# The first reading of k and v for their bounds: flat 2 KB rows in place of rows by key and head

## The chip, the cores and the metric

The kernel runs on one core of one Trainium2 chip. The metric is the device time of one execution in microseconds (us); of several runs the median is given.

## What is computed

```python
def _attn_ref(q, k, v, f):
    B, H, S, D = q.shape                      # 4, 8, 576, 64
    scores = np.matmul(q, k.transpose(0, 1, 3, 2)) / np.sqrt(D)
    cum = np.cumsum(np.log(np.clip(f, 0.0001, 1.0)), axis=-1)
    scores = np.where(causal, -1e9, scores + cum[..., :, None] - cum[..., None, :])
    attn = softmax(scores)
    return np.matmul(attn, v)

def _moe_ref(x, w_in, w_out):                 # 2304 x 512, 512 x 2048, 2048 x 512
    h = x @ w_in
    return (h * np.tanh(np.log1p(np.exp(h)))) @ w_out

def _moe2_ref(x, w_in, w_out, g_ln):          # d_ff 1024
    h = x @ w_in
    solu = h * softmax(h)
    return (layernorm(solu) * g_ln) @ w_out

def reference(...):
    x = _attn_ref(q, k, v, f).transpose(0, 2, 1, 3).reshape(B * S, H * D)
    return _moe2_ref(_moe_ref(x, ...), ...)
```

All is in float32. The kernel splits each operand of a product into a high and a low part in float16, scaled by a power of two that comes from a bound on the operand, and adds three products.

## The kernel before, in words

Three stages run one into the other. The attention goes batch by batch (`b` 0 to 3), in five chunks `i` of up to 128 queries each and in groups of heads; one step takes a group through scores (PE, L436 to L441), maximum and exponential (DVE L483 and L496, ACT L485, L499, L500), the split into two float16 parts (`step_h`, L523 and L524), a DMA transpose `pT<-ph` (L529) and the product with v (PE, L555 to L557). The first feed-forward layer takes blocks of 256 tokens as they come out: `up` (PE, L785), the activation (`mish_a`, `mish_b`, `mish_c`), `down` (PE, L829). The second layer (`Stage2`) starts when the last attention step is issued; its products are L1028 and L1068. Each batch has 576 keys; batches 1 to 3 lie in the 128-row chunks with an offset of 64, so that chunk 0 has 64 rows there and chunk 4 has 128.

The scale of a batch's k and v must be known before its first chunk is split, so k and v are read twice. The first reading is for the bounds alone: for each chunk `c` a load (`load_raw(b + 1, c, "kv")`), and an activation Square with a running sum on ACT (`stats`, L316), which writes one column of the small tile `st`; `scales` (L332) takes the maximum over the columns, adds over the partitions with a product by ones (L329), and forms the scales. The second reading loads q, k and v of a chunk again (`load_raw(nb, ni, "qkv")`) for the split (`split_k`, `split_v`, `split_q`). Batch 0 is read once, into other buffers.

`load_raw` (L292) puts one key into one partition: from the array [batch, head, key, 64] it takes, for each of up to 128 keys, eight pieces of 64 floats (256 bytes), one per head:

```python
            i = nc.sync.dma_start(
                t[r0:r1_].rearrange("p (h d) -> p h d", h=H),
                src[b, :, t0:t0 + n, :].rearrange("h s d -> s h d"),
            )
```

The tiles of both readings come from one pool, `rawp`, with three buffers of 128 x 512 floats that go round in the order of the program; a load waits until the tile three before it has been used. `ahead` (L645) places the loads of the first reading of batch `b + 1` in the attention of batch `b`, at the steps n = 6, 8, 14, 15, 16 counted over heads and chunks from chunk 2 on, and the Squares at n = 8, 10, 15, 16, 17; `scales` follows at n = 18.

All loads, stores and transposes are issued from SP's queue, in order. A scheduler sets each engine's row of instructions from the program's order, the dependences and its own estimates of durations; inside an engine the row is kept at run time.

Of the kernel before, what the change touches and what calls it, by code (L numbers as in the profile page):

```python
# [8 lines left out]
F32 = mybir.dt.float32  # L9
# [3 lines left out]
AF = mybir.ActivationFunctionType  # L13
# [5 lines left out]
P = 128  # L19
B, H, S, D = 4, 8, 576, 64  # L20
DM = H * D
# [52 lines left out]
def rows_of(b, c):  # L74
    off = OFF[b]
    lo = max(128 * c, off)
    hi = min(128 * c + 128, off + S)
    return lo - 128 * c, hi - 128 * c, lo - off
# [130 lines left out]
def emit(tc, q, k, v, f, w_in, w_out, w2_in, w2_out, g_ln, out):  # L209
    nc = tc.nc  # L210
# [39 lines left out]
    rawp = ea.enter_context(tc.tile_pool(name="rawp", bufs=RB, side="right"))  # L250
# [35 lines left out]
    raw = {}  # L286
    sc = {}
# [4 lines left out]
    def load_raw(b, c, which, pool=None):  # L292
        r0, r1_, t0 = rows_of(b, c)
        n = r1_ - r0
        for nm in which:
            src = {"q": q, "k": k, "v": v}[nm]
            if pool is None:
                t = rawp.tile([P, DM], F32, tag="raw", name=f"raw{nm}_{b}_{c}")
            else:
                t = pool.pop()  # L300
            raw[nm, b, c] = t
# [3 lines that stand above are left out]
            )  # L305
        return i

    def stats(b, c, which):

        if ("st", b) not in sc:  # L310
            sc["st", b] = att.tile([P, 2, NCH], F32, tag="st", name=f"st_{b}", bufs=2)
            nc.vector.memset(sc["st", b], 0.0)
        r0, r1_, _ = rows_of(b, c)
        for nm in which:
            jk = attd.tile([P, DM], F32, tag="x32", name=f"jk{nm}_{b}_{c}", bufs=1)
            nc.scalar.activation(  # L316
                jk[r0:r1_], raw[nm, b, c][r0:r1_], AF.Square,
                accum_out=sc["st", b][r0:r1_, "kv".index(nm), c:c + 1])
# [13 lines left out]
    def scales(b, which):  # L332

        j0 = "kv".index(which[0])
        n = len(which)
        t = att.tile([P, 6, 2], F32, tag="sct", name=f"sct{which}_{b}", bufs=1)
        x = [t[:, i, :n] for i in range(6)]
        nc.vector.tensor_reduce(x[0], sc["st", b][:, j0:j0 + n], axis=AX.X, op=ALU.max)
        src = across(x[0], x[1])
        nc.vector.tensor_scalar(x[1], src, 2.0 ** -40, None, op0=ALU.max)  # L340
        root2(nc, x[4], x[1])
        nc.vector.reciprocal(x[5], x[4])
        for i, nm in enumerate(which):
            pw, ip = t[:, 4, i:i + 1], t[:, 5, i:i + 1]
            if nm == "k":
                u = att.tile([P, 2], F32, tag="scu", name=f"scu_{b}", bufs=2)
                c = 64.0
                nc.vector.tensor_scalar(u[:, 0:1], pw, 0.125 / c, None, op0=ALU.mult)
                nc.vector.tensor_scalar(u[:, 1:2], ip, c, None, op0=ALU.mult)
                sc["q", b], sc["k", b] = u[:, 0:1], u[:, 1:2]  # L350
            else:
                u = att.tile([P, 1], F32, tag="scv", name=f"scv_{b}", bufs=2)
                nc.vector.tensor_scalar(u, ip, 2.0 ** 14, None, op0=ALU.mult)
                nc.vector.tensor_scalar(iv[b], pw, 2.0 ** -14, None, op0=ALU.mult)
                sc["v", b] = u
# [9 lines left out]
    def split_k(b, c):  # L365
        r0, r1_, t0 = rows_of(b, c)
        n = r1_ - r0
        t = kn[cnt["kn"] % KNB]
        cnt["kn"] += 1
        t3 = t[:, :H * P].rearrange("p (h d) -> p h d", h=H)  # L370
        rk = hd(raw["k", b, c][r0:r1_])
        s = sc["k", b][r0:r1_]
        split(nc, t3[r0:r1_, :, 64:], t3[r0:r1_, :, :64], rk, s, qmode(b, c, 0))
        kc = ktr[:, (b * NCH + c) % NKT]
        kt[b, c] = kc
        nc.sync.dma_start_transpose(out=kc[:, :H, r0:r1_], in_=t[r0:r1_, :H * P])
        nc.vector.tensor_copy(kc[:64, H:, r0:r1_], kc[64:, :H, r0:r1_])
        nc.sync.dma_start(
            kc[64:67, H:, r0:r1_],
            dd[b * H:(b + 1) * H, :, t0:t0 + n].rearrange("h j s -> j h s"),  # L380
        )

    def split_v(b, c):
        r0, r1_, _ = rows_of(b, c)
        vc = attd.tile([P, 2, DM], F16, tag="vt", name=f"vt_{b}_{c}", bufs=6)
        vt[b, c] = vc
        rv = raw["v", b, c][r0:r1_]
        s = sc["v", b][r0:r1_]
        split(nc, vc[r0:r1_, 0], vc[r0:r1_, 1], rv, s, qmode(b, c, 1))

    def split_q(b, c):
        r0, r1_, t0 = rows_of(b, c)
        t = attd.tile([P, H, P], F16, tag="qn", name=f"qn_{b}_{c}", bufs=1)
        rq = hd(raw["q", b, c][r0:r1_])
        s = sc["q", b][r0:r1_]
        split(nc, t[r0:r1_, :, :64], t[r0:r1_, :, 64:], rq, s, qmode(b, c, 2))
        qa = attd.tile([P, H, P], F16, tag="qa", name=f"qa_{b}_{c}", bufs=2)
        pend["qt"] = nc.sync.dma_start_transpose(out=qa[:, :, r0:r1_], in_=t[r0:r1_].rearrange("p h d -> p (h d)"))
        qb_ = qb[cnt["qb"] % 2]
        cnt["qb"] += 1  # L400
        nc.vector.tensor_copy(qb_[:64, :, r0:r1_], qa[:64, :, r0:r1_])  # L401
        qt[b, c] = (qa, qb_)
# [242 lines left out]
    def ahead(b, i, h):  # L645

        nb, ni = (b, i + 1) if i + 1 < NCH else (b + 1, 0)
        if b + 1 < B and i in (2, 3, 4):
            n = (i - 2) * H + h
            if n in (6, 8, 14, 15, 16):  # L650
                load_raw(b + 1, (6, 8, 14, 15, 16).index(n), "kv")
            if n in (8, 10, 15, 16, 17):
                stats(b + 1, (8, 10, 15, 16, 17).index(n), "kv")
            if n == 18:
                scales(b + 1, "kv")
        if nb < B:
            if h == (LD if ni else 3) and nb > 0:
                load_raw(nb, ni, "qkv")
            if h == LD and nb == 0 and ni >= 3:
                load_raw(nb, ni, "q")  # L660
            if h == (LD + 2 if ni else 4):
                if nb or ni > 1:
                    split_k(nb, ni)
                    split_q(nb, ni)
                split_v(nb, ni)
# [20 lines left out]
    def slot_pe():  # L686
        n = pos["k"]
        if n < len(seq):
            step_s(*seq[n])
            b, i, hs = seq[n]  # L690
            for h in hs:
                ahead(b, i, h)
        pvs(n - LAG)
        pos["k"] += 1
# [10 lines left out]
    for x in range(len(order) + WPF):  # L705
        if WPF <= x < len(order):
            wsteps.append((order[x][0].load, order[x][1]))
        if x >= WPF:
            w, n = order[x - WPF]
# [28 lines left out]
    for c in range(NCH):  # L738
        stats(0, c, "k")
# [9 lines left out]
    for c in range(NCH):  # L749
        stats(0, c, "v")  # L750
# [124 lines left out]
    for j in range(NBLK):  # L875
        last = (j + 1) * TB - 1
        b, t = divmod(last, S)
# [28 lines left out]
    for hn in range(2 * (NF + 5)):  # L906
        n, half = divmod(hn, 2)
# [212 lines left out]
```

## Time and profile before

| | |
|---|---|
| median of 3 runs | 859.61 us (858.01 to 860.01) |
| profiled execution | span 856.0 us from the first to the last instruction; its own time is not listed, the median is 3.6 us above its span |
| busy PE, DVE, ACT, POOL | 739.0, 617.6, 548.2, 440.8 us |
| DMA | 328568 packets, 114.83 MB, 317676 of them under 512 bytes |
| mean granted clock of TensorE | 0.977 of full speed |

Busy times are of one engine each and overlap. A busy PE is not a PE at its peak. The DMA share of a stretch is the mean busy share of 16 DMA engines; it can pass 1 where packets overlap. In the chain of waits each piece is what released the next one; "issue" is time in which an engine waited for nothing that the profile shows. SPq is SP's queue, which issues DMAs.

### The profile page before, as it was taken

To read this page: it belongs to the slowest core of one execution; us is meant where nothing else is said; L and a number is where in the kernel's file an instruction comes from. 1 tells how busy PE (TensorE), PEld (TensorE's weight loads), DVE (VectorE), ACT (ScalarE), POOL (GpSimd) and SP (SyncE) were. 2 spreads that over 40 slices of the span, in tenths; PEclk is the share of its full clock that TensorE was granted. 3 is DMA by queue.
4 is the path that set the end of the run, shared out by engine and by line. 5 is a ranking of instruction groups with operands and counts; after the bars stand their busy time and mean duration, and the time that the engine had idled before them with its cause. 6 is when DMAs were issued, how large, how long until landed. Compare 5 with 4: busy or idle time off the path is not lost.

```text
span 856.0 us, 15746 instructions
## 1 busy us (share of the span) xinstructions
PE 739.0 (86%) x5822; PEld 456.4 (53%) x5822; DVE 617.6 (72%) x1158; ACT 548.2 (64%) x1202; POOL 440.8 (51%) x341
## 2 busy tenths in 40 slices
PE   0545776689999999997999999986999999999998
PEld 0334543447656666575666767553555554444443
DVE  6799999498867989769896755599566444665551
ACT  5645647868779877877877767686855554333331
POOL 2268676755976667755678653128832222022110
PEclk9999997889999999999999999999999999999999
DMA  9999555477899898988897533941013323344443
GB/s 239 229 215 281 160 176 94 93 137 145 153 174 190 168 169 153 184 155 153 173 180 119 115 70 63 233 156 61 26 38 87 74 64 73 87 101 106 104 88 82
DMA packets 328568, 114.83 MB, mean 134 GB/s; under 512 B 317676, under 2 KB 317676, under 8 KB 328492
## 3 DMA queue, kind: packets, MB, share of 16 engines
q1 hardware_dynamic: 328492, 113.84, 63.9%
q8 instruction: 45, 0.74, 0.4%
q14 instruction: 31, 0.25, 0.1%
HBM read 46.59 MB, written 9.55 MB: 66 GB/s over the span
## 4 chain that ended last, share of the span: by engine, by line
PE 37%; DVE 24%; DMA 12%; ACT 11%; issue 8%; POOL 6%; SPq 1%; DVEq 0%; ACTq 0%; POOLq 0%
PE h L1028 11%; PE o L1068 10%; PE x L829 7%; PE h L785 6%; DMA pT<-ph 3%; POOL ph L524 3%; DVE th L806 2%; DVE ta L802 2%; ACT p L485 2%; DVE ph L521 1%; DMA w2i_r<-in_moe_w_in_dram 1%; DMA ktr<-kn 1%; DMA rawk<-in_k_dram 1%; ACT p L500 1%; DVE nm L483 1%
## 5 line engine op out<-in xcount | busy, mean ns | idle before, releaser
L829 PE MATMUL x<-wout,gt 128*128 128x512 f16 x864 | 219.8, 387 | 18.2 <-ACT gt L811 8.8
L785 PE MATMUL h<-xT,win 128*128 128x256 f16 x1728 | 221.2, 277 | 2.3 <-POOL win L203 1.7
L524 POOL TENSOR_TENSOR ph<-p,ph 128x512 f16<-128x512 f32 (+4 forms) x120 | 157.0, 1314 | 81.3 <-ACT ph L523 35.0
L785 PEld LDWEIGHTS <-win 128*128 128x128 f16 x1728 | 168.5, 100 | 45.8 <-POOL win L203 1.8
L812 POOL TENSOR_TENSOR gt<-th,gt 128x512 f16<-128x512 f32 x72 | 92.4, 1284 | 106.5 <-ACT gt L811 105.3
L829 PEld LDWEIGHTS <-gt 128*128 128x128 f16 x864 | 80.0, 100 | 99.3 <-ACT gt L811 11.6
L1056 POOL TENSOR_TENSOR z<-sl,z 128x1024 f16<-128x1024 f32 x18 | 38.7, 2151 | 138.0 <-DVE s2c L1035 111.1
L1028 PE MATMUL h<-w,x2T 128*128 128x512 f16 x432 | 98.4, 380 | 2.9 <-POOL w L206 1.6
L1068 PE MATMUL o<-wo,zT 128*128 128x512 f16 x432 | 96.5, 379 | 0.5 <-DMA zT<-z 0.5
L555 PE MATMUL pv<-vt,pT 128*128 128x64 f16 (+3 forms) x480 | 71.4, 203 | 23.0 <-DMA pT<-ph 20.2
L806 DVE SCALAR_TENSOR_TENSOR th<-ta,th 128x512 f32<-128x512 f32 x72 | 71.9, 1000 | 24.7 <-ACT ta L805 24.4
L485 ACT ACTIVATE p<-sp,nm 64x64 f32<-64x64 f32 (+7 forms) x128 | 61.3, 484 | 38.7 <-DVE nm L483 21.1
L436 PE MATMUL sp<-ktr,qa 128*128 128x64 f16 (+6 forms) x304 | 59.6, 253 | 22.8 <-ACT p L485 8.7
L811 ACT CAST gt<-th 128x512 f16<-128x512 f32 x72 | 44.3, 615 | 50.2 <-DVE th L806 49.9
L802 DVE TENSOR_SCALAR ta<-ta 128x512 f32<-128x512 f32 x72 | 58.8, 816 | 20.4 <-ACT ta L797 19.9
L1028 PEld LDWEIGHTS <-x2T 128*128 128x128 f16 x432 | 42.3, 98 | 53.9 <-issue 4.0
L555 PEld LDWEIGHTS <-pT 128*128 128x128 f16 (+3 forms) x480 | 45.4, 101 | 47.9 <-DMA pT<-ph 31.3
L556 PE MATMUL pv<-vt,pT 128*128 128x64 f16 (+3 forms) x480 | 70.4, 198 | 0.6 <-DVE vt L199 0.6
L557 PE MATMUL pv<-vt,pT 128*128 128x64 f16 (+3 forms) x480 | 70.2, 198 | 0.0
L1068 PEld LDWEIGHTS <-zT 128*128 128x128 f16 x432 | 42.2, 98 | 51.5 <-DMA zT<-z 1.0
L437 PE MATMUL sp<-ktr,qb 67*128 67x64 f16 (+6 forms) x304 | 63.3, 254 | 3.6 <-DVE qb L401 3.6
L1039 ACT ACTIVATE e<-h,s2c 128x1024 f32<-128x1024 f32 x18 | 21.7, 1204 | 68.1 <-DVE s2c L1037 68.1
(235 smaller groups left out, 1443.5 us busy)
## 6 DMA issues: line engine op xcount, KB each, us to landing
wi_r<-in_moe_w_in_dram SPq DMA_DIRECT2D x8, 1024.0 KB
wo_r<-in_moe_w_out_dram SPq DMA_DIRECT2D x8, 1024.0 KB
rawk<-in_k_dram SPq DMA_DIRECT2D x25, 256.0 KB
rawv<-in_v_dram SPq DMA_DIRECT2D x25, 256.0 KB
x2d<-x2h SPq DMA_DIRECT2D x18, 256.0 KB
out_dram<-ro SPq DMA_DIRECT2D x18, 256.0 KB
w2i_r<-in_moe_w_in_dram SPq DMA_DIRECT2D x4, 1024.0 KB
w2o_r<-in_moe_w_out_dram SPq DMA_DIRECT2D x4, 1024.0 KB
```

Source lines behind the costliest of these rows:

```text
L485: nc.scalar.activation(pv[:m, g * (i + 1) * P + off:g * (i + 1) * P + end], s3[:, g, off:end], AF.Exp, bias=nm[:m, g:g + 1], accum_out=rs[ ...
L524: nc.gpsimd.tensor_tensor(p4[:, :, 1], pv3, p4[:, :, 0], op=ALU.subtract)
L555: nc.tensor.matmul(o, pT[a0:a1, k, :m], vh, start=(c == 0), stop=False)
L556: nc.tensor.matmul(o, pT[a0:a1, k, :m], vl, start=False, stop=False)
L557: nc.tensor.matmul(o, pT[a0:a1, k + 1, :m], vh, start=False, stop=(c == i))
L785: nc.tensor.matmul(ph, win[:, (fi // 4) * NC1 + c, col:col + P], x[:, lx * NC1 + c, :], start=(m == 0), stop=(m == 3 * NC1 - 1))
L802: nc.vector.tensor_scalar(ta, ta, E20, 1.0, op0=ALU.min, op1=ALU.add)
L806: nc.vector.scalar_tensor_tensor(th, ta, 2.5, th, op0=ALU.subtract, op1=ALU.mult)
L812: nc.gpsimd.tensor_tensor(gt[:, 1], th, gt[:, 0], op=ALU.subtract)
L829: nc.tensor.matmul(o, gt[:, lg, n % 2, t * P:(t + 1) * P], wout[:, fi, lw * 512:(lw + 1) * 512], start=(first and m == 0), stop=(last and ...
L1028: nc.tensor.matmul(h[:, half * 512:(half + 1) * 512], x[:, lx * NC1 + c, :], self.w2[:, half * NC1 + c, lw * 512:(lw + 1) * 512], start=(n ...
L1068: nc.tensor.matmul(o, zT[:, lz * NF2 + c, :], self.wo[:, c, lw * 512:(lw + 1) * 512], start=(n == 0), stop=(n == 3 * NF2 - 1))
```

## The change

The first reading of batches 1 to 3 no longer goes by key and head. `load_flat` takes the batch's 294912 floats of k (or v) as 128 pieces of 2304 consecutive floats, one per partition, and loads 512 columns of that at a time: four loads of 128 rows of 2 KB, and a last one of 128 rows of 1 KB. The Square runs on all 128 partitions over 512 (the last one 256) columns, into one column of `st`. The loads and Squares are called at the same steps, from the same three buffers. The second reading and batch 0 stay.

```diff
+    def load_flat(b, c):
+
+        n = min(DM, H * S * D // P - c * DM)
+        for nm, src in (("k", k), ("v", v)):
+            t = rawp.tile([P, DM], F32, tag="raw", name=f"flat{nm}_{b}_{c}")
+            raw[nm, b, -1 - c] = t[:, :n]
+            nc.sync.dma_start(
+                t[:, :n], src[b].rearrange("h s d -> (h s d)").rearrange("(p x) -> p x", p=P)[:, c * DM:c * DM + n])
+
+    def stats_flat(b, c):
+        stats(b, c, "kv", True)
+
-    def stats(b, c, which):
+    def stats(b, c, which, flat=False):
...
             jk = attd.tile([P, DM], F32, tag="x32", name=f"jk{nm}_{b}_{c}", bufs=1)
+            if flat:
+                x = raw.pop((nm, b, -1 - c))
+                nc.scalar.activation(
+                    jk[:, :x.shape[-1]], x, AF.Square, accum_out=sc["st", b][:, "kv".index(nm), c:c + 1])
+                continue
...
             if n in (6, 8, 14, 15, 16):
-                load_raw(b + 1, (6, 8, 14, 15, 16).index(n), "kv")
+                load_flat(b + 1, (6, 8, 14, 15, 16).index(n))
             if n in (8, 10, 15, 16, 17):
-                stats(b + 1, (8, 10, 15, 16, 17).index(n), "kv")
+                stats_flat(b + 1, (8, 10, 15, 16, 17).index(n))
```

Lines of the changed kernel behind L307 stand 12 to 17 further down (L529 is L546 there). The scheduler's order changes with it, from the first of these loads on. Two places, both where the end of batch 2's chunk 3 meets batch 3's first reading. In the rows, `raw` or `flat`, then k, v or q, then the chunk names a load (the numbers behind are buffer names); `pT_3_6` is the transpose for heads 6 and 7 of chunk 3, and `ktr<-dd` loads a part of the decay.

SP's row before, from the transpose pT_3_4 on:

```order
L529 DMA_TRANSPOSE pT_3_4_4614<-ph_3_4_4557 128x16x128
L302 DMA rawk_3_4682<-in_k_dram 128x8x64
L302 DMA rawv_3_4684<-in_v_dram 128x8x64
L302 DMA rawk_4_4746<-in_k_dram 128x8x64
L529 DMA_TRANSPOSE pT_3_6_4710<-ph_3_6_4660 128x16x128
L302 DMA rawv_4_4748<-in_v_dram 128x8x64
L302 DMA rawq_0_4943<-in_q_dram 64x8x64
L302 DMA rawk_0_4945<-in_k_dram 64x8x64
L378 DMA ktr<-dd 3x8x128
L302 DMA rawv_0_4947<-in_v_dram 64x8x64
```

and with the change, from the load flatv_3 on:

```order
L314 DMA flatv_3_4684<-in_v_dram 128x512
L314 DMA flatk_4_4746<-in_k_dram 128x256
L546 DMA_TRANSPOSE pT_3_4_4614<-ph_3_4_4557 128x16x128
L314 DMA flatv_4_4748<-in_v_dram 128x256
L302 DMA rawq_0_4943<-in_q_dram 64x8x64
L302 DMA rawk_0_4945<-in_k_dram 64x8x64
L395 DMA ktr<-dd 3x8x128
L302 DMA rawv_0_4947<-in_v_dram 64x8x64
L546 DMA_TRANSPOSE pT_3_6_4710<-ph_3_6_4660 128x16x128
```

The transpose pT_3_6 stood ahead of the first reading's last load, rawv_4; now it stands behind that load and behind rawq_0, rawk_0 and rawv_0 of the second reading.

ACT's row at the same place before, from the exponential of head 6 of chunk 3 on (`p` with nm_3_6, head 7 with nm_3_7; `jkk_3` and `jkv_3` are the Squares of the first reading's chunk 3):

```order
L485 ACTIVATE p_0_129,rsum_3_4363<-sp_149,nm_3_6_4657 128x448
L797 ACTIVATE ta_4690<-h_10_4593,usc_1_80 128x512
L798 ACTIVATE th_4691<-h_10_4593,ths 128x512
L485 ACTIVATE p_1_130,rsum_3_4363<-sp_147,nm_3_7_4700 128x448
L803 ACTIVATE ta_4690<-ta_4690 128x512
L804 ACTIVATE ta_4690<-ta_4690,c_k_72 128x512
L805 ACTIVATE ta_4690<-ta_4690 128x512
L316 ACTIVATE jkk_3_4750,st_4321<-rawk_3_4682 128x512
L811 CAST gt_4778<-th_4691 128x512
L316 ACTIVATE jkv_3_4752,st_4321<-rawv_3_4684 128x512
L499 ACTIVATE p_0_129,rsum_4_4787<-sp_149,nm_4_0_4788 128x64
L500 ACTIVATE p_0_129,rsum_4_4787<-sp_147,nm_4_0_4788 128x512
```

and with the change, from the Square of flatk_3 on:

```order
L330 ACTIVATE jkk_3_4750,st_4321<-flatk_3_4682 128x512
L502 ACTIVATE p_0_129,rsum_3_4363<-sp_149,nm_3_6_4657 128x448
L330 ACTIVATE jkv_3_4752,st_4321<-flatv_3_4684 128x512
L814 ACTIVATE ta_4690<-h_10_4593,usc_1_80 128x512
L815 ACTIVATE th_4691<-h_10_4593,ths 128x512
L330 ACTIVATE jkk_4_4815,st_4321<-flatk_4_4746 128x256
L502 ACTIVATE p_1_130,rsum_3_4363<-sp_147,nm_3_7_4700 128x448
L820 ACTIVATE ta_4690<-ta_4690 128x512
L330 ACTIVATE jkv_4_4817,st_4321<-flatv_4_4748 128x256
L821 ACTIVATE ta_4690<-ta_4690,c_k_72 128x512
L822 ACTIVATE ta_4690<-ta_4690 128x512
```

The Squares of chunks 3 and 4 stood behind head 7's exponential of chunk 3 and among the exponentials of chunk 4 (L499, L500; now L516, L517); now that of flatk_3 stands ahead of head 6's, and all four ahead of chunk 4.

## Rows read from the trace of the kernel before

**Rows 1.** The page: the span and each engine's busy time.
```profile
span 856.0 us, 15746 instructions
...
PE 739.0 (86%) x5822; PEld 456.4 (53%) x5822; DVE 617.6 (72%) x1158; ACT 548.2 (64%) x1202; POOL 440.8 (51%) x341
```

**Rows 2.** Busy time by stretch: length, engines (instructions), PE's clock, DMA share, GB/s.
```profile
360.00:380.00 20.00, 19.57 (x222) 13.68 (x223) 11.42 (x18) 15.16 (x38) 13.01 (x12) 1.00 1.02 190
...
130.00:460.00 330.00, 294.62 (x2958) 198.26 (x2958) 266.05 (x488) 260.25 (x641) 227.11 (x197) 0.96 0.84 154
600.00:840.00 240.00, 240.00 (x1244) 121.41 (x1242) 133.00 (x327) 111.29 (x207) 65.90 (x40) 1.00 0.35 77
```

**Rows 3.** Chain of waits from 130 to 460 us: shares, then two of its longest pieces.
```profile
by line: issue 12.7%; DMA pT<-ph 8.5%; POOL ph L524 5.9%; PE x L829 5.8%; PE h L785 5.6%; DMA ktr<-kn 3.6%; DVE th L806 2.6%; DVE ph L521 2.5%; ACT p L485 2.4%; DMA qa<-qn 2.3%; POOL gt L812 2.2%; DVE ta L802 2.2%; PE pv L555 1.9%; ACT p L5
...
340.85 5.00 DMA rawv<-in_v_dram
...
367.56 5.21 DMA rawk<-in_k_dram
```

**Rows 4.** Waits of PE from 130 to 460 us: total, times, longest.
```profile
PE pv L555 <- DMA pT<-ph: 16.5, 18, 2.5
```

**Rows 5.** The page: DMA packets of the execution.
```profile
DMA packets 328568, 114.83 MB, mean 134 GB/s; under 512 B 317676, under 2 KB 317676, under 8 KB 328492
```

**Rows 6.** Busy time by stretch, columns as in rows 2, near the start.
```profile
4.00:9.00 5.00, 0.00 (x0) 0.00 (x0) 4.27 (x6) 3.84 (x8) 1.32 (x3) 1.00 1.34 203
12.00:15.00 3.00, 0.00 (x0) 0.00 (x0) 1.74 (x4) 3.00 (x5) 0.00 (x0) 1.00 1.02 408
```

**Rows 7.** ACT's timeline: Squares of batches 1 to 3 that waited for loads.
```profile
151.19 0.63 ACT L316 ACTIVATE jkv<-rawv 128x512 f32<-128x512 f32 x1 [1.07 <-DMA rawv<-in_v_dram]
...
242.31 0.63 ACT L316 ACTIVATE jkv<-rawv 128x512 f32<-128x512 f32 x1 [0.91 <-DMA rawv<-in_v_dram]
...
263.19 0.63 ACT L316 ACTIVATE jkk<-rawk 128x512 f32<-128x512 f32 x1 [0.35 <-DMA rawk<-in_k_dram]
...
362.87 0.63 ACT L316 ACTIVATE jkk<-rawk 128x512 f32<-128x512 f32 x1 [0.46 <-DMA rawk<-in_k_dram]
...
363.75 0.63 ACT L316 ACTIVATE jkv<-rawv 128x512 f32<-128x512 f32 x1 [0.15 <-DMA rawv<-in_v_dram]
...
372.78 0.63 ACT L316 ACTIVATE jkk<-rawk 128x512 f32<-128x512 f32 x1 [3.20 <-DMA rawk<-in_k_dram]
```

**Rows 8.** SP's timeline: start, us of issue; around batch 1's and batch 3's loads.
```profile
101.30 0.37 SPq L302 DMA_DIRECT2D rawk<-in_k_dram  x1
...
142.26 0.53 SPq L302 DMA_DIRECT2D rawv<-in_v_dram  x1
...
367.56 0.94 SPq L302 DMA_DIRECT2D rawk<-in_k_dram  x1
368.58 0.74 SPq L302 DMA_DIRECT2D rawv<-in_v_dram  x1
369.43 1.76 SPq L302 DMA_DIRECT2D rawk<-in_k_dram  x1
371.29 3.27 SPq L529 DMA_TRANSPOSE pT<-ph  x1
374.65 0.53 SPq L302 DMA_DIRECT2D rawv<-in_v_dram  x1
...
381.04 0.59 SPq L302 DMA_DIRECT2D rawv<-in_v_dram  x1
```

**Rows 9.** Groups of ACT by shape: busy us, mean ns, idle before and releaser.
```profile
L797 ACT ACTIVATE ta<-h,usc 128x256 f32<-128x256 f32 x16 | 6.7, 476 | 0.0
...
L316 ACT ACTIVATE jkv<-rawv 64x512 f32<-64x512 f32 x4 | 2.5, 628 | 0.1
L316 ACT ACTIVATE jkk<-rawk 64x512 f32<-64x512 f32 x4 | 2.5, 628 | 0.3 <-DMA rawk<-in_k_dram 0.2
```

**Rows 10.** Tile rawv: SP's issue of its loads, ns shortest/median/longest.
```profile
L302 SPq DMA_DIRECT2D rawv<-in_v_dram x32: 367/597/1702, 29.9 to 441.1; - x32
```

**Rows 11.** PE's timeline: first product of heads 6 and 7, chunk 3, batch 2.
```profile
377.74 0.20 PE L555 MATMUL pv<-vt,pT 64*128 64x64 f16 x1
```

## The prediction

> **What bounds the kernel now.** I first read the page's busy times: PE 739.0 us of a span of 856.0 us, DVE 617.6, ACT 548.2, POOL 440.8 [rows 1]. PE is the bound where it has no gaps: from 600 to 840 us it is busy 240.00 of 240 us [rows 2], so what is won or lost before 600 us reaches the end unchanged, and nothing can be won after it. The first readings of batches 1 to 3 are spread over the attention of batches 0 to 2; the last load of batch 3's goes out at 374.65 us [rows 8]. From 130 to 460 us PE is busy 294.62 of 330 us, so 35.4 us of gaps are the most that stretch could give back, while the DMA engines are 0.84 busy and ACT and DVE 260 and 266 us [rows 2]. In that stretch the chain of waits has the transfers pT (8.5%), ktr (3.6%) and qa (2.3%), transposes all, in 14.4% of 330 us, some 47 us [rows 3]; by the waits of PE itself, its longest is the product with v for pT, 16.5 us in 18 times [rows 4]. Two of the five longest pieces of the chain are loads that the change touches: rawv at 340.85 (5.00 us) and rawk at 367.56 (5.21 us), both of batch 3's first reading by their place in SP's order [rows 3]. So the stretch is limited by latencies that run through the DMA queue as much as by PE, and the changed loads stand in that queue.
>
> **What the change removes.** Before, one chunk of k or v is 128 keys x 8 heads rows of 256 bytes, 1024 packets; batches 1 to 3 have 24 such loads and 6 of half the size. After, there are 24 loads of 128 rows of 2 KB and 6 of 128 rows of 1 KB. The bytes stay: 27 loads' worth of 256 KB. Packets go from 27 x 1024 = 27648 to 30 x 128 = 3840, so of 328568 packets [rows 5] 304760 should be left. The cost of each part:
>
> (a) **The transfer.** While only loads of 256-byte rows run (4 to 9 us) the DMA engines, busy throughout, move 203 GB/s; while only weights in 4 KB rows run (12 to 15 us) they move 408 GB/s [rows 6]. 256 KB (262144 bytes) so take 1.29 us against 0.64 us. Rows of 2 KB are not in the trace as loads by themselves; a load can cost from 0.64 (as 4 KB rows) to 1.29 us (no gain). 2 KB is eight times the old row and half of the weights' row, so I take 0.65 us saved: 27 x 0.65 = 17.5 us of DMA time, with zero as the other end. The Trainium skill (DMA: Bandwidth & Descriptors, Why small descriptors are slow) puts the loss at 3 cycles beside the 8 that a 256-byte descriptor needs; by that, 2 KB rows would cost 67 cycles for 88, a quarter less in place of half, and the saving would be an estimated 8 us over all 27. The trace does not agree that the loss of the 256-byte rows is so small, 203 against 408 GB/s.
>
> (b) **ACT's waits for these loads.** Before its Squares of batches 1 to 3 ACT sat idle for these loads six times, 1.07 + 0.91 + 0.35 + 0.46 + 0.15 + 3.20 = 6.14 us [rows 7]. One transfer is 0.65 us shorter, but the loads come in pairs and threes behind each other [rows 8], so I take half, 3.1 us less; the ends are 0 and 6.1. ACT is not the bound there: from 360 to 380 us, around the longest of these waits, PE is busy 19.57 of 20 us [rows 2]. So I let half of that half reach the end: **1.5 us**, between 0 and 6.1.
>
> (c) **What queues behind the loads.** From 130 to 460 us the DMA engines are busy 0.84 x 330 = 277 us. Batch 1's first seven loads (up to its rawk_3, at 101.30 us, the next being at 142.26 [rows 8]), six full ones' worth, go before that; the other 21 take 13.6 us off it, about 5%. If the chain's 47 us of transposes shorten by the same share, that is 2.3 us; by PE's own 16.5 us it is 0.8. I take **2 us**, with 0 and 6 as ends: the busy share is so near 1 in places (1.02 from 360 to 380 us [rows 2]) that queueing can fall by more than in proportion.
>
> (d) **The Squares.** Six Squares of 64 partitions x 512 (628 ns) become 128 x 256, and an activation of 128 x 256 took 476 ns [rows 9], so 6 x 0.15 = 0.9 us of ACT. Where ACT waits for data this is hidden, and if ACT were the bound it would be the 0.9 us: I count 0.
>
> (e) **SP's issue.** An issue of these loads takes 367 ns at least and 597 in the median [rows 10]. The flat ones have two dimensions for three; 30 x 0.23 = 6.9 us of SP's time could go, or nothing. SP waits for its sources most of the time, so this counts 0, covered by those waits.
>
> (f) **The order.** The scheduler now takes the loads to land sooner and has moved rows on all five engines; from about 480 us on (the last third of PE's rows) the order is as it was. At the places that I show, Squares stand earlier in ACT's row and a transpose stands later in SP's row. For the rest I have no sign, so 0, with 4 us to either side, which is the size of the single waits that such a move makes or removes (2.5 us was the longest of PE's for pT [rows 4], 3.20 the longest of ACT's [rows 7]).
>
> **The sum.** -1.5 - 2 = -3.5 us against the profiled execution. Its span is 856.0 us; the median of the three runs shown, 859.61, is 3.6 us more, which lies outside the first and last instruction and is not changed. So the span should be 852.5 and the time **856.1**, which I round to 856.0. A measurement of this kernel can tell about 0.3% (2.6 us) from no change, so "faster" begins at 857.0 and "slower" at 862.2: the forecast is only just on the faster side.
>
> **Rivals.**
> 1. *Hidden.* The loads land earlier, but PE in-order and DVE hold the pace, as the 19.57 of 20 us around the longest wait say [rows 2]. Then (b) gives 0 and (c) at most the 0.8 that is proportionate for PE: 858.8 to 859.6, say 859. Against it: the gaps of PE for pT, 16.5 us, are real and hang on the DMA queue.
> 2. *The queue drains.* With a DMA share of 1.02 around the longest wait [rows 2], taking away 5% of the work may cut queueing by far more than 5%. If half of PE's 16.5 us for pT went (8.2) and the 1.5 of (b) with it, the time would be 859.6 - 9.7 = 850. Against it: a transpose's own transfer stays, and the chain's part of POOL, DVE and ACT too.
> 3. *Slower: the order counts on loads that do not land so early.* In batch 3, SP issued pT_3_6 at 371.29, ahead of rawv_4; its product on PE began at 377.74, while rawv_0 went only at 381.04 [rows 8, 11]. Now pT_3_6 stands behind rawv_0, and rawv_0 takes the buffer that ACT's Square of flatv_4 gives back. If the loads take as long as before, pT_3_6 goes some 9.8 us later (381.04 - 371.29), and PE, which takes its rows in order, waits. pT_3_6's issue takes 3.27 us, so its transfer ended at 374.6 or later, and of the 9.8 us at most 3.2 are covered (377.74 - 374.56): a loss of some 7 us, of which (b) and (c) return 2: 859.6 + 5 = 864.5. It decides once flatv_4's Square ends later than 3.2 us after the point where pT_3_6 could have been issued before. For it: ACT's Squares of chunks 3 and 4 now stand before the exponentials of heads 6 and 7, and the wait of 3.20 us there would stand in front of these. Against it: those Squares are earlier too, so the buffers come free earlier by design, and the last two loads in question carry half as much (chunk 4 has 1 KB a row).
> 4. *The rows are cut again.* If rows of 2 KB went out as 256-byte packets, the count would stay at 328568 and (a) be 0. The page counts packets of 2 KB and more already (328492 under 8 KB against 317676 under 2 KB [rows 5]), so I give it nothing of its own; it would look like rival 1, at 859.6.
>
> **How the numbers follow.** The forecast has 0.42: with (f) its values spread over 850 to 860; of the 0.42, 0.30 lies under 857.0 and 0.12 within 0.3%. Rival 2 has 0.15, all faster. Rival 1 has 0.20: 0.15 same, 0.03 faster and 0.02 slower. Rival 3 has 0.23: 0.20 slower and 0.03 same. That makes faster 0.48, same 0.30, slower 0.22. The range reaches from 847 (3 us under rival 2's value, since the half of PE's wait that it takes is a choice) to 864.5 (rival 3's value), which leaves about a tenth at either end. The likeliest case's own range is 850 to 860.
>
> **What would show it.** Right: 304760 packets; DMA share from 130 to 460 us down from 0.84 to about 0.79; ACT's idle time in front of the Squares of batches 1 to 3 near 3 us in place of 6.1; PE's wait for pT under 16.5 us; from 600 us on the same lines, only earlier. Rival 1: the first three, but PE's gaps from 130 to 460 us still 35 us. Rival 3: a wait of PE for pT of 5 us or more in one piece near 370 to 385 us, with SP standing at a load of q, k or v in front of it. The prediction would be wrong in its foundation if the DMA share did not fall, that is if 2 KB rows went no faster than rows of 256 bytes, or if PE's gaps grew in a part of the program where no first reading stands.

## The result, and the profile after

| | before | changed |
|---|---|---|
| median | 858.95 us (858.01 to 860.01, 4 runs) | 868.01 us (865.95 to 868.81, 4 runs) |
| ratio | | 1.0101, 95% interval 1.0084 to 1.0119 |
| span of the profiled execution | 856.0 us | 864.1 us |

The change makes the kernel 1.0% slower. The forecast was 856.0 us, range 847.0 to 864.5: the time lies outside it, on the other side of no change.

The page of the changed kernel, its span, busy times and packets:

```profile
span 864.1 us, 15781 instructions
...
PE 746.5 (86%) x5822; PEld 461.7 (53%) x5822; DVE 614.7 (71%) x1158; ACT 547.7 (63%) x1202; POOL 437.0 (51%) x341
...
DMA packets 304760, 114.83 MB, mean 133 GB/s; under 512 B 290028, under 2 KB 290796, under 8 KB 304684
```

The packets are what was worked out, 304760 against 328568 [rows 5]. PE has the same 5822 products and is busy 7.5 us longer [rows 1].

Busy time by stretch of the changed kernel (columns as in rows 2):

```profile
130.00:460.00 330.00, 293.32 (x2900) 198.37 (x2897) 259.29 (x480) 254.41 (x629) 224.81 (x192) 0.95 0.80 149
...
380.00:400.00 20.00, 20.00 (x180) 13.69 (x179) 12.73 (x34) 13.09 (x32) 9.71 (x8) 0.95 0.61 93
...
600.00:840.00 240.00, 239.06 (x1244) 121.79 (x1242) 137.19 (x329) 114.61 (x211) 71.38 (x43) 0.99 0.34 75
```

The DMA share from 130 to 460 us is 0.80 against 0.84 [rows 2]. That alone shows no relief: run 2 below, which has the old rows of 256 bytes and the changed kernel's order, is at 0.81 there too. A kernel that runs late has less of its work in this stretch.

```profile
130.00:460.00 330.00, 289.92 (x2845) 196.26 (x2843) 254.16 (x472) 252.57 (x621) 218.24 (x186) 0.94 0.81 149
```

What the transfers gave is read further down, under (a), from the whole execution. From 600 us on PE is still busy almost without a gap. So the 8.1 us of span were lost earlier.

PE's waits for pT in that stretch, and ACT's idle time ahead of the Squares (tiles flatk and flatv: total us, times), all of the changed kernel:

```profile
PE pv L572 <- DMA pT<-ph: 16.6, 18, 2.9
```

```profile
  DMA flatk<-in_k_dram: 0.6, 1
...
  DMA flatv<-in_v_dram: 4.8, 6
```

PE waits as long for pT as before, 16.6 against 16.5 us [rows 4], and ACT 5.4 us for the loads against 6.14 [rows 7]. The chain of waits from 130 to 460 us gives pT more of the time, 10.2% against 8.5% [rows 3]:

```profile
by line: issue 10.4%; DMA pT<-ph 10.2%; PE h L802 8.3%; PE x L846 6.5%; POOL ph L541 6.4%; DMA ktr<-kn 3.6%; PE pv L572 2.9%; POOL ph L536 2.6%; DMA rawq<-in_q_dram 2.6%; DMA qa<-qn 2.6%; POOL gt L829 2.3%; DVE ta L819 2.3%; DVE th L823 2.2
```

**Where the time went.** The cast of a finished attention chunk on DVE (L573 before, L590 after; 20 in all) is a milestone that both kernels pass. Three of the 20, those of chunk 3 of batches 1 and 2 and the last of all, in the timeline of DVE of the kernel before:

```profile
275.57 1.20 DVE L573 CAST xh<-x 128x512 f16<-128x512 f32 x1
...
382.72 0.41 DVE L573 CAST xh<-x 128x512 f16<-128x512 f32 x1
...
531.08 0.42 DVE L573 CAST xh<-x 128x512 f16<-128x512 f32 x1
```

and of the changed kernel:

```profile
280.02 0.41 DVE L590 CAST xh<-x 128x512 f16<-128x512 f32 x1
...
389.90 0.42 DVE L590 CAST xh<-x 128x512 f16<-128x512 f32 x1
...
539.82 0.42 DVE L590 CAST xh<-x 128x512 f16<-128x512 f32 x1
```

The delay is 4.5, 7.2 and 8.7 us: it builds up over the attention of batches 1 to 3, though not steadily. At the milestone that stood at 254 us before it is 0.2 us, at those at 423 and 432 us 3.7 us. What PE lost there can be read off the stretches 200 to 420 and 420 to 610 us; before:

```profile
200.00:420.00 220.00, 202.97 (x2094) 139.17 (x2093) 181.07 (x327) 177.33 (x450) 154.18 (x139) 0.99 0.92 166
420.00:610.00 190.00, 172.43 (x1487) 115.58 (x1485) 138.88 (x227) 139.05 (x279) 106.94 (x87) 0.99 0.54 120
```

and after:

```profile
200.00:420.00 220.00, 203.00 (x2043) 139.28 (x2040) 174.53 (x314) 172.65 (x439) 154.40 (x137) 0.97 0.89 166
420.00:610.00 190.00, 170.12 (x1486) 113.87 (x1487) 141.69 (x238) 137.36 (x288) 102.86 (x86) 0.98 0.57 125
```

Idle time is the length less PE's busy time: 17.0 + 17.6 = 34.6 us before, 17.0 + 19.9 = 36.9 after, 2.3 more. Busy time times what is missing of the granted clock: 203.0 x 0.01 + 172.4 x 0.01 = 3.8 us before, 203.0 x 0.03 + 170.1 x 0.02 = 9.5 after, 5.7 more (the clock is rounded, so within 2 us or so either way). Together 8.0 us, as much as the span grew. Only this sum can be relied on, not how it divides. Run 1 below loses no time, and the same working of its two rows gives 14.3 + 15.1 = 29.4 us idle and 4.1 + 5.2 = 9.4 us for the clock: as much for the clock as in the changed kernel, but 38.8 us together, against 38.4 before and 46.4 in the changed kernel. One place where the changed kernel has a pause and a low clock behind it, in its timeline of PE and by stretch:

```profile
377.25 0.20 PE L572 MATMUL pv<-vt,pT 64*128 64x64 f16 x1 [2.38 <-DMA pT<-ph]
```

```profile
374.00:377.00 3.00, 0.87 (x18) 0.62 (x16) 1.78 (x5) 2.02 (x6) 1.13 (x2) 1.00 0.77 164
377.00:383.00 6.00, 5.75 (x46) 3.45 (x47) 1.61 (x4) 3.22 (x9) 2.80 (x4) 0.72 0.67 133
```

PE was busy 0.87 of 3 us, and then had a granted clock of 0.72 over the next 6 us: a mixture of its two levels, 1.2 and 2.4 GHz.

### The profile page after: what moved, and what is told of

It reads as the page before. It is cut to its first block, busy times and chain, and to the rows that moved or that the text cites. A ratio compares the mean times of both kernels' runs of the same rounds, so it can differ in the third digit from the quotient of the medians.

```text
span 864.1 us, 15781 instructions
## 1 busy us (share of the span) xinstructions
PE 746.5 (86%) x5822; PEld 461.7 (53%) x5822; DVE 614.7 (71%) x1158; ACT 547.7 (63%) x1202; POOL 437.0 (51%) x341
## 2 busy tenths in 40 slices
DMA packets 304760, 114.83 MB, mean 133 GB/s; under 512 B 290028, under 2 KB 290796, under 8 KB 304684
## 4 chain that ended last, share of the span: by engine, by line
PE 39%; DVE 21%; DMA 14%; ACT 9%; POOL 7%; issue 7%; SPq 1%; DVEq 0%; POOLq 0%; ACTq 0%
PE h L1045 10%; PE o L1085 10%; PE x L846 8%; PE h L802 7%; DMA pT<-ph 5%; POOL ph L541 3%; DVE ta L819 2%; DVE th L823 2%; DMA w2i_r<-in_moe_w_in_dram 1%; DMA ktr<-kn 1%; PE pv L572 1%; DVE wout L139 1%; POOL gt L829 1%; DVE win L139 1%; ACT p L502 1%
## 5 line engine op out<-in xcount | busy, mean ns | idle before, releaser
L802 PE MATMUL h<-xT,win 128*128 128x256 f16 x1728 | 226.2, 282 | 3.8 <-ACT th L815 1.9
L802 PEld LDWEIGHTS <-win 128*128 128x128 f16 x1728 | 171.7, 101 | 50.0 <-issue 4.8
L541 POOL TENSOR_TENSOR ph<-p,ph 128x512 f16<-128x512 f32 (+4 forms) x120 | 152.5, 1277 | 89.2 <-ACT ph L540 38.8
L829 POOL TENSOR_TENSOR gt<-th,gt 128x512 f16<-128x512 f32 x72 | 94.8, 1318 | 98.8 <-ACT gt L828 98.7
L820 ACT ACTIVATE ta<-ta 128x512 f32<-128x512 f32 x72 | 45.3, 631 | 43.0 <-DVE ta L819 43.0
L573 PE MATMUL pv<-vt,pT 128*128 128x64 f16 (+3 forms) x480 | 69.9, 198 | 0.6 <-DVE vt L199 0.6
L819 DVE TENSOR_SCALAR ta<-ta 128x512 f32<-128x512 f32 x72 | 55.9, 776 | 19.2 <-ACT ta L814 18.8
```

The source lines that it names most:

```text
L541: nc.gpsimd.tensor_tensor(p4[:, :, 1], pv3, p4[:, :, 0], op=ALU.subtract)
L573: nc.tensor.matmul(o, pT[a0:a1, k, :m], vl, start=False, stop=False)
L802: nc.tensor.matmul(ph, win[:, (fi // 4) * NC1 + c, col:col + P], x[:, lx * NC1 + c, :], start=(m == 0), stop=(m == 3 * NC1 - 1))
L819: nc.vector.tensor_scalar(ta, ta, E20, 1.0, op0=ALU.min, op1=ALU.add)
L829: nc.gpsimd.tensor_tensor(gt[:, 1], th, gt[:, 0], op=ALU.subtract)
```

## Experiments

Theory A: the flat loads are good, and the new order of the engines' rows is what costs. Theory B: the flat loads themselves cost. To part them, a kernel can be held to another kernel's order. `pin` takes that order as a list and makes each instruction of the named rows depend on the one ahead of it in the list, for the order of issue alone; what is computed, loaded and waited for is not touched.

```diff
+def pin(tc, engines):
+    for e in engines:
...
+            if last is not None:
+                tc.add_manual_dep(
+                    i, last.name,
+                    mybir.DependencyInfo(mybir.DependencyClass.NoSync, mybir.DependencyReason.DATA),
+                    reason="issue order")
+            last = i
...
         emit(tc, *args, o)
+        pin(tc, ["PE", "DVE", "Activation", "Pool", "SP"])
```

All ratios below are to the kernel before, run beside them, whose median was between 857.9 and 859.6 us.

**1. Flat loads, old order on all five engines** (the diff above on the changed kernel).

> The changed kernel (flat loads), with every engine's row of instructions pinned to the order of the kernel before. Theory A (the new order costs the time, by PE's gaps and the low clock that follows them): 854 to 859 us, at or under the kernel before, DMA share from 130 to 460 us about 0.80 as with the change. Theory B (the flat loads themselves cost, by what 2 KB rows do to the transposes beside them): 865 us or more, as the changed kernel.

Measured: 857.74 us (12 runs), ratio 0.9983 (0.9969 to 0.9996). Faster than both kernels, if by little against the kernel before. The DMA share from 130 to 460 us is 0.81. The same stretches and milestones, flat loads in the old order:

```profile
200.00:420.00 220.00, 205.66 (x2108) 141.52 (x2104) 182.49 (x328) 176.86 (x458) 155.09 (x140) 0.98 0.88 167
420.00:610.00 190.00, 174.91 (x1494) 116.56 (x1495) 138.90 (x227) 139.70 (x280) 106.21 (x86) 0.97 0.52 119
```

```profile
275.74 1.20 DVE L590 CAST xh<-x 128x512 f16<-128x512 f32 x1
...
382.44 0.41 DVE L590 CAST xh<-x 128x512 f16<-128x512 f32 x1
...
532.13 0.42 DVE L590 CAST xh<-x 128x512 f16<-128x512 f32 x1
```

The milestones stand within 1.1 us of those before. In this order the flat loads do what they were forecast to do to PE's wait for pT from 130 to 460 us, 16.5 us before [rows 4]:

```profile
PE pv L572 <- DMA pT<-ph: 12.1, 15, 1.8
```

**2. Rows of 256 bytes, new order on all five engines** (the same edit on the kernel before, with the changed kernel's order).

> The kernel before (rows of 256 bytes by key and head), with every engine's row pinned to the order of the changed kernel. Theory A: 866 to 872 us, the changed kernel's time or a little more, since the loads land later than the order counts on. Theory B: about 859 us, as the kernel before.

Measured: 871.61 us (5 runs), ratio 1.0143 (1.0120 to 1.0167). Runs 1 and 2 make a square of two by two: the new order costs 1.0101 / 0.9983, 1.2% or 10 us, with flat loads and 1.4% or 12 us without; the flat loads save 0.2% (1.5 us) in the old order and 0.4% (3.6 us, from 1.0143 to 1.0101) in the new. Theory B falls.

**3 and 4. Flat loads, one row alone held to the old order**: SP's, then PE's. The scheduler orders the rest anew.

```diff
+        pin(tc, ["SP"])
```

> The changed kernel with SP's row alone pinned to the old order; the scheduler sets the others anew round it. If the transposes that went behind loads in SP's row are what costs (rival 3 of the prediction): 855 to 861 us. If it is the order on PE, ACT or DVE: 864 us or more.

Measured: 871.28 us (4 runs), 1.0142 (1.0125 to 1.0160).

> The changed kernel with PE's row alone pinned to the old order. If the order of scores, products with v and feed-forward products on PE is what costs: 855 to 861 us. If it lies in SP's or ACT's row: 864 us or more.

Measured: 870.93 us (4 runs), 1.0130 (1.0106 to 1.0155). Neither row alone brings the time back.

**5. Is it the flat loads' shorter transfers that lead the scheduler astray, or does any edit here do it?** The kernel before, v asked for ahead of k, nothing else.

```diff
-                load_raw(b + 1, (6, 8, 14, 15, 16).index(n), "kv")
+                load_raw(b + 1, (6, 8, 14, 15, 16).index(n), "vk")
```

> The kernel before (256-byte rows, first reading as it was) with one harmless edit: at the first reading v is asked for ahead of k. The work and the transfers are the same to the byte; the scheduler draws a new order from it. If the order before was a favourable draw that any edit at this place loses (theory A1), the time is 866 to 873 us, like the other redrawn orders (868.0, 870.9, 871.3, 871.6). If it is the shorter flat transfers, as the scheduler sees them, that lead it to a worse order (theory A2), this kernel stays at 857 to 862 us. If the flat loads themselves cost (theory B), it stays at 859 to 860 us too.

Measured: 870.12 us (4 runs), 1.0132 (1.0106 to 1.0158). This is within theory A1: an edit that changes neither work nor bytes costs as much as the change did. But it is not as harmless as its forecast calls it. The Squares still take k first, and k is now asked for second; ACT's waits ahead of them from 90 to 460 us, all for k (us, times, longest), are 10.4 us, where all six waits for k and v made 6.14 before [rows 7]:

```profile
ACT jkk L316 <- DMA rawk<-in_k_dram: 10.4, 6, 2.5
```

So a part of the loss may come of this and not of the order. Its milestones, 9.0 and 14.4 us behind those before:

```profile
284.54 1.20 DVE L573 CAST xh<-x 128x512 f16<-128x512 f32 x1
...
545.49 0.42 DVE L573 CAST xh<-x 128x512 f16<-128x512 f32 x1
```

**6. The same edit on the changed kernel.**

```diff
-        for nm, src in (("k", k), ("v", v)):
+        for nm, src in (("v", v), ("k", k)):
```

> The changed kernel with the same harmless edit: flat loads, v ahead of k. Theory A1: another draw, somewhere between 857 and 873 us, most likely 864 to 872 us, and some us off the changed kernel's 868.0. Theory A2: 866 to 872 us, since the transfers are as short as in the changed kernel. Theory B (the flat loads cost by themselves): 868 us.

Measured: 870.38 us (4 runs), 1.0143 (1.0115 to 1.0171): within A1 and A2 both, 2 us over what B said. Here too k's Squares wait, 9.5 us, where the changed kernel's waits were 5.4.

**9. The control to 5: k and v swapped in the loads and in the Squares.** Then the rows of PE, DVE and POOL come out as before.

```diff
-                load_raw(b + 1, (6, 8, 14, 15, 16).index(n), "kv")
+                load_raw(b + 1, (6, 8, 14, 15, 16).index(n), "vk")
...
-                stats(b + 1, (8, 10, 15, 16, 17).index(n), "kv")
+                stats(b + 1, (8, 10, 15, 16, 17).index(n), "vk")
```

> The kernel before with k and v swapped at the first reading in the loads and in the Squares alike. The rows of PE, DVE and POOL stay word for word those of before; SP's and ACT's rows differ only in that k and v stand in each other's place. If what costs is the new order of the engines' work (theory A), this kernel takes 857 to 861 us although it is the same kind of edit as the one that took 870.1. If the edit itself (v ahead of k) is what costs, it takes 866 to 872 us.

Measured: 858.61 us (10 runs), 1.0007 (0.9994 to 1.0019). With loads and Squares in step again and the rows of PE, DVE and POOL as before, the time is as before. This run takes away both the new order of run 5 and its longer waits for k, so it doesn't tell the two apart. That an order by itself costs rests on runs 1 and 2.

**7 and 8. Where in the program?** Flat loads; the old order for the steps written ahead of batch 2's first reading alone, then for those from there on alone.

```diff
-            if i is None:
+            if i is None or n >= 2552:    # 7; in 8: n < 2552
```

> The changed kernel with every engine's row held to the order of before for all steps written ahead of batch 2's first reading (some 215 us of the run); the rest is the scheduler's own. If the loss comes of the order at batch 1's first reading (theory A-early), the time is 857 to 861 us; if it comes of the order at batches 2 and 3 (theory A-late), 865 to 872 us; a new tail is another draw in any case, so a time between the two is possible.

Measured: 865.67 us (6 runs), 1.0087 (1.0059 to 1.0115).

> The changed kernel with every engine's row held to the order of before for all steps written from batch 2's first reading on, the head free. Theory A-early: 862 to 870 us, since the head's new order leaves its loss behind. Theory A-late: 857 to 861 us.

Measured: 863.86 us (6 runs), 1.0066 (1.0046 to 1.0086). Neither end: each part loses by itself, as far as two halves with a seam between them can tell. By the three milestones, run 8 is 4.5, 4.3 and 5.1 us late, so it loses early and then keeps pace; run 7 is 1.1, 3.3 and 8.2 us late.

**10 and 11. Which engines?** Flat loads; old order on all but SP, then on PE and DVE alone.

```diff
+        pin(tc, ["PE", "DVE", "Activation", "Pool"])    # 10; in 11: ["PE", "DVE"]
```

> The changed kernel with the rows of PE, DVE, ACT and POOL held to the order of before and SP's row free: the DMAs alone are in a new order. If the compute engines' order decides (theory A-compute), 857 to 861 us. If the place of the DMAs in SP's row decides (theory A-SP; it is what my rival with pT behind a load meant), 864 to 872 us.

Measured: 862.00 us (6 runs), 1.0050 (1.0029 to 1.0072): between the two. SP's new row alone costs 0.7% against run 1, some 6 us.

> The changed kernel with the rows of PE and DVE held to the order of before, ACT, POOL and SP free. PE's row alone gave 870.9. If it is PE's order against DVE's that has to fit, 857 to 862 us; if ACT's or SP's new order costs by itself, 864 to 872 us.

Measured: 874.96 us (4 runs), 1.0194 (1.0165 to 1.0224), worse than with no row held. A row of the old order beside rows of another is no help.

**12. Rival 3 by itself.** Flat loads, old order, and in SP's row two transposes alone moved to where the changed kernel has them:

```diff
-L546 DMA_TRANSPOSE pT_3_4
 L314 DMA flatk_3
 L314 DMA flatv_3
 L314 DMA flatk_4
-L546 DMA_TRANSPOSE pT_3_6
+L546 DMA_TRANSPOSE pT_3_4
 L314 DMA flatv_4
 L302 DMA rawq_0
 L302 DMA rawk_0
 L395 DMA ktr<-dd
 L302 DMA rawv_0
+L546 DMA_TRANSPOSE pT_3_6
```

> The changed kernel with the old order on all engines (857.7 us), and in SP's row two DMAs alone put where the changed kernel has them: pT_3_4 behind flatk_3, flatv_3 and flatk_4 of batch 3's first reading, and pT_3_6 behind rawv_0. This is my rival 3 by itself. If that is a main part of the 10.3 us between this order and the new one (theory A-place), 861 to 866 us; rival 3 priced it at 7 us. If the loss is spread over many places of the order, of which this is one (theory A-spread), 857 to 860 us.

Measured: 866.41 us (6 runs), 1.0105 (1.0086 to 1.0124), a little above the range of theory A-place. Two DMAs out of some 15700 instructions cost 1.0105 / 0.9983, 1.2% (10 us; 8.7 by the bare medians of runs 12 and 1). By the three milestones this run is 0.6 us early, then 7.9 and 9.5 us late, so the loss arises here. SP's timeline of this run, then ACT's Square of flatv_4 and PE's two waits:

```profile
374.15 0.45 SPq L395 DMA_DIRECT2D ktr<-dd  x1
381.90 0.59 SPq L302 DMA_DIRECT2D rawv<-in_v_dram  x1
382.55 5.99 SPq L546 DMA_TRANSPOSE pT<-ph  x2
```

```profile
381.38 0.41 ACT L330 ACTIVATE jkv<-flatv 128x256 f32<-128x256 f32 x1
```

```profile
372.21 0.20 PE L572 MATMUL pv<-vt,pT 64*128 64x64 f16 x1 [2.75 <-DMA pT<-ph]
...
387.55 0.23 PE L572 MATMUL pv<-vt,pT 64*128 64x64 f16 x1 [6.25 <-DMA pT<-ph]
```

SP stands from 374.6 to 381.9 us at rawv_0, until ACT's Square of flatv_4 gives its buffer back; pT_3_6 goes behind it, and PE waits 6.25 us. Busy time by stretch there shows what else that pause costs:

```profile
382.00:388.00 6.00, 0.45 (x7) 0.37 (x8) 0.45 (x2) 0.40 (x1) 1.25 (x1) 0.64 0.88 160
388.00:394.00 6.00, 6.00 (x39) 3.55 (x37) 1.70 (x4) 1.58 (x5) 2.84 (x3) 0.51 0.39 75
```

PE is idle for 5.5 of 6 us, and the next 6 us run at the lower clock, 0.51.

**14. The first of the two alone**, pT_3_4 behind flatk_4.

> The old order with flat loads (857.7 us), and of the two late transposes of the run that took 866.4 only the first, pT_3_4 behind flatk_4. If the wait of 6.25 us that stood at pT_3_6 carries the loss, 857 to 860 us; if the wait of 2.75 us at pT_3_4 and the low clock behind it carry half, 861 to 863 us.

Measured: 858.66 us (12 runs), 1.0011 (0.9995 to 1.0026), 0.3% or 2 us over run 1. PE's wait for it was 2.5 us here too. By the difference, the late pT_3_6 carries most of run 12's loss: 1.0105 / 1.0011, 0.9% or 8 us. It was not moved alone.

**13. The two put back in the changed kernel's own order**, all other places held to that order.

> The changed kernel held to its own order on every engine, with two DMAs of SP's row alone put back: pT_3_4 ahead of flatk_3 of batch 3's first reading, pT_3_6 behind flatk_4 of it and so ahead of rawv_0. If these two places cost the changed kernel its 10 us too (theory A-place), 858 to 862 us. If its loss is spread over the order (theory A-spread), 865 to 869 us: its longest wait of PE for pT here was 2.38 us and no more, and PE was busy without a gap from 380 to 400 us.

Measured: 874.67 us (4 runs), 1.0194 (1.0173 to 1.0215). Neither theory: what costs 1.2% when it is moved back in the old order costs another 0.9% when it is moved forward in the new. SP's timeline shows what happens there, then ACT's and PE's:

```profile
366.34 9.26 SPq L546 DMA_TRANSPOSE pT<-ph  x2
375.71 0.82 SPq L314 DMA_DIRECT2D flatk<-in_k_dram  x1
```

```profile
379.20 0.63 ACT L330 ACTIVATE jkk<-flatk 128x512 f32<-128x512 f32 x1 [4.37 <-DMA flatk<-in_k_dram]
```

```profile
380.59 0.21 PE L453 MATMUL sp<-ktr,qa 128*128 128x64 f16 x1 [2.92 <-ACT p L502]
...
383.93 0.26 PE L453 MATMUL sp<-ktr,qa 128*128 128x128 f16 x1 [2.17 <-ACT p L502]
```

SP stands at two transposes from 366.34 to 375.6 us, flatk_3 goes behind them, and ACT, whose row in this order has that Square ahead of an exponential, waits 4.37 us; PE waits for the exponentials in turn. This execution was 3.9 us behind the changed kernel's at the milestone ahead of this place already and 11.1 us at the one behind it, so some 7 us arise here.

## Why the prediction was wrong

**What bounds the kernel** held in the main. The last milestone is 8.7 us late and the span 8.1 longer: what is lost before 600 us reaches the end. Two readings in the working were wrong. The 35.4 us of gaps are not all that the stretch from 130 to 460 us can give or take: its granted clock was 0.96 [rows 2], and the sum has no term for the clock. And of the 3.6 us between span and median about half was no time outside the instructions: the changed kernel's profiled execution took 865.95 us with a span of 864.1, 1.8 us more, so the execution profiled before was faster than the median. This does not change the sum.

**(a) The transfer** held in kind and was taken somewhat too large. The page gives the time of all packets of the main queue as a share of 16 engines' span (packets, MB, share). The kernel before and run 1, both in the old order:

```profile
q1 hardware_dynamic: 328492, 113.84, 63.9%
q1 hardware_dynamic: 304684, 113.84, 62.3%
```

Run 2 and the changed kernel, both in the new order:

```profile
q1 hardware_dynamic: 328492, 113.84, 62.7%
q1 hardware_dynamic: 304684, 113.84, 62.1%
```

Times the spans, 856.0, 856.7, 873.5 and 864.1 us, that is 547 and 534 us in the old order, 548 and 537 in the new: 11 to 13 us less for 27 loads' worth, 0.4 to 0.5 us a load, where I had 0.65. By the Trainium skill's figures (DMA: Bandwidth & Descriptors, Why small descriptors are slow) it would have been an estimated 0.3 us a load; the traces lie above that.

**(b) and (c), ACT's waits and the queue**, were about right as a sum: -3.5 us forecast, -1.5 measured in the old order (interval -2.7 to -0.3) and -3.6 in the new one. ACT's waits in run 1 were 3.6 us, near the 3.1 forecast, and PE's wait for pT fell by 4.4 us, of which only a part reached the end.

**(d) and (e)** were not tried by themselves; the -1.5 of run 1 contains them.

**(f), the order, is the step that failed.** It said 0, with 4 us to either side, "the size of the single waits that such a move makes or removes". Measured, it is +10 us with the flat loads and +12 without. The zero was wrong: of seven orders that the scheduler drew anew after an edit at this place or with some rows held (runs 3 to 6, 10 and 11 and the changed kernel), all seven were slower than the order before, by 0.5 to 1.9%. The evidence for a favourable order before is not seven free draws, though: runs 3, 4, 10 and 11 hold some rows to another order, and runs 5 and 6 make k's Squares wait. That any new order at this place loses is therefore likely and not shown. The size was wrong too: one place alone made 10 us (run 12 against run 1), where PE's longest wait for pT in the trace of before was 2.5 us [rows 4]: the wait there was 6.25 us, and the lower clock came behind it; and the new order loses in several places (runs 7 and 8), so its losses add up.

**Rival 3** had its mechanism right and its part in the changed kernel wrong. Run 12 is that mechanism as it was priced, at the place and with the signs named: a wait of 6.25 us in one piece at 387.55, SP standing at rawv_0 until the Square of flatv_4 was done; 7 us forecast for it, some 10 measured. But the changed kernel moved PE's and ACT's rows along with SP's. There the Square of flatv_4 is done earlier, so SP reaches pT_3_6 sooner:

```profile
370.56 0.33 SPq L314 DMA_DIRECT2D flatk<-in_k_dram  x1
371.06 2.81 SPq L546 DMA_TRANSPOSE pT<-ph  x1
...
378.15 0.60 SPq L302 DMA_DIRECT2D rawv<-in_v_dram  x1
378.80 2.17 SPq L546 DMA_TRANSPOSE pT<-ph  x1
```

PE has other work until it lands (busy 20.00 of 20 us from 380 to 400, first section), and the 2.38 us at 377.25 are for pT_3_4. That its 864.5 us came nearest to 868.0 is chance. **Rival 4** is out by the packets; **rivals 1 and 2** spoke of an order that stays, and run 1 lies between the forecast and rival 1.

Of the signs listed, the packets came true; the DMA share came down as far as said, but it does so without flat loads too (run 2). ACT's idle time (5.4 for 3 us) and PE's wait for pT (16.6) did not come true. PE's idle time between 420 and 610 us, where no first reading stands, grew from 17.6 to 19.9 us, which looks like the sign that I had named for a wrong foundation. It does not count as one: part of it is the delay (the stretch from 428 to 618 us has 18.8), and run 1, in the order of before, has 15.1 there, so single executions differ by as much.

Open: what makes the order before better than the seven others, as a property of the order. No run here tells it, and none shows that it is the best. Nor does one tell which places of the changed kernel's order carry its loss: putting the two transposes of rival 3 back did not bring it back (run 13). Open too is how the 8.0 us divide between PE's pauses and its lower clock, and what the low clock behind a pause costs by itself; no run holds the one and changes the other.

## What to carry to other kernels

Where a scheduler sets the order, an edit is two changes: its own, and a new order; hold the old order on all engines to measure the first, and hold the old kernel to the new order to measure the second. An edit that moves no work is a weaker control: see first that no step waits longer for its load by it, as in run 5. Where other orders of the same kernel have been measured and lose, price a new order as such a loss, not as zero; here they cost 0.5 to 1.9%, and what they cost in another kernel no run here shows. If the edit is worth having, keep it with the old order: the flat loads in the old order are the fastest version here, 0.9983 of before and 1.2% under the changed kernel; but hold all rows or none, since one or two rows held beside new ones did no better than none.

## What was not expected of the hardware

A low clock of TensorE can be free. From 60 to 120 us the profiled run of experiment 1 had a granted clock of 0.76:

```profile
60.00:120.00 60.00, 41.23 (x314) 28.23 (x313) 58.14 (x76) 33.69 (x61) 46.46 (x26) 0.76 0.70 198
```

and that of the kernel before 0.95:

```profile
60.00:120.00 60.00, 40.11 (x313) 26.89 (x312) 59.47 (x76) 33.71 (x61) 47.58 (x26) 0.95 0.75 198
```

DVE is busy 58 to 59 of 60 us there and PE 40 to 41, so PE is not what sets the pace. The milestones behind it, at 138, 178 and 275 us, stand 0.8, 1.9 and 0.2 us later than before. The mean clock of run 1's profile is the lowest of all, 0.942, and that execution took 858.43 us, less than the median of the kernel before. From 200 to 610 us, where PE has few gaps, run 1 has 9.4 us for the clock by the account above, as much as the changed kernel, and 5.2 us less idle time of PE than the kernel before; its last milestone stands 1.1 us later. So in this run the share of the clock times PE's busy time is not what the clock cost: most of it came out of PE's gaps.
